# Layer 1 of an MLP in Strassen's seven products, on one Trainium2 core

## The chip, the core and the metric

The kernel runs on one core of a Trainium2 chip. The core has a matrix engine (PE, TensorE; its weight loads are shown apart as PEld), a vector engine (DVE), a scalar engine (ACT), a general engine (POOL, GpSimd) and a queue that issues the DMAs (SP). The metric is the device time of one execution in microseconds (us). Numbers of the profile come from one profiled execution.

## What is computed

Performer attention, a low-rank mixing of tokens, and a relu MLP with a residual; all in float32, with the weights given in float64.

```python
# q, k, v: (8 batches, 8 heads, 576 tokens, 64); omega: (128, 64)
phi(x) = exp(h - max(h)) / sqrt(m)        # h = scaled x @ omega^T - |x|^2 / 2
attn = phi(q) (phi(k)^T v) / (phi(q) sum(phi(k)) + 1e-6)
x = attn as (8, 576, 512)
u = x + (x^T U V)^T                       # U: (576, 32), V: (32, 576)
out = u + relu(u @ w1) @ w2               # w1: (512, 2048), w2: (2048, 512)
```

## The kernel before

The 8 x 576 rows make 36 tiles of 128 tokens. The program has three stages: the attention and the mixing, which write u to DRAM (tensors `u_dram`); a first part of the MLP during which the float64 weights are still decoded (five DVE instructions, two of POOL and two of ACT for each of 32 pieces of 512 columns, lines 111 to 163); and the rest of the MLP with all weights in place. The MLP is the larger part of the program.

A float32 product on PE is made of three passes over operands that are split into a rounded high part and a remainder (float32r): high x high, low x high, high x low. A split is a cast on ACT and a subtraction on POOL. `w1` is kept split for good in `w1h` and `w1l`, `w2` in `w2s`.

The MLP takes u in 12 chunks of three tiles (384 tokens; `CT = 3`, class `Chunk`). For a chunk, 32 x 32 blocks are fetched from `u_dram` by 16 DMAs into four buffers `uraw` (line 327), turned on DVE into `uT` (line 672), cast on ACT into `uh` (675) and subtracted on POOL into `ul` (676). An item is a chunk c and a block f of 128 of the 2048 hidden columns (16 blocks):

- `layer1`: 12 matmuls of 384 columns into one PSUM bank `p_p` (lines 682 to 684), then relu on ACT into `gh` (687) and the remainder on DVE into `gl` (688);
- `layer2`: for each of three tiles three matmuls of 512 columns, summed over all f in the chunk's own banks (700).

PE does `layer1` of the next item before `layer2` of this one, so `gh` and `gl` have a whole layer 2 in which to be made. Chunks 0 and 1 share the pass over f while the weights are decoded. At a chunk's end DVE adds the residual rows of u (716), which SP has loaded into buffers of their own half a chunk earlier (711), and SP stores them (717).

The order on each engine is fixed when the program is built: a list scheduler of the framework places each instruction by its own estimate of times; only the instructions marked with `keep_in_program_order` hold the order of the source among themselves. Each engine then takes its instructions strictly in that order.

Of the kernel before, what the change touches and what calls it, by code (L numbers as in the profile page):

```python
# [23 lines left out]
#: High words of the least and the greatest float64 with a normal float32's exponent.  # L24
# [4 lines left out]
def performer_mlp_kernel(ctx: ExitStack, tc, q, k, v, omega, U, V, w1, w2, out):  # L29
    """phi(q) (phi(k)^T v) / den, then x + V^T U^T x and a relu MLP with a residual.  # L30

    float32 products run natively or as float32r passes over operands split exactly into a
    rounded high part and the remainder. U, V, w1 and w2 come as the bits of float64 and are
    rounded to float32. The 2 x 576 rows of a pair of batches make nine tiles of 128, the fifth
    with the last 64 rows of one batch and the first 64 of the next.
    """
    nc = tc.nc
# [16 lines left out]
    # Both feature maps carry 1 / sqrt(M), which the quotient drops when the guard grows by M.  # L54
# [12 lines left out]
    CT = 3  # L67
    NCH = NP * NT // CT
    TOK = CT * P
    u_dram = [dram.tile([TOK, DM], F32, name=f"u_dram{i}") for i in range(NCH)]  # L70
# [26 lines left out]
    def decoding(jobs, late=0):  # L97
        """jobs: (load, n, finish...); load(raw) fills [P, n, 2] with the words of n float64 in each
        row, and each finish(w) runs in turn on the float32 [P, n]. Yields after every VectorE
        instruction; loads run ahead."""  # L100
# [18 lines left out]
        for i, job in enumerate(jobs):  # L119
# [4 lines left out]
            # The float32 of the high word's bits in m; the rest is the low word in units of 2^-52  # L124
            # of its power of two.
# [40 lines left out]
    def w1_job(i):  # L166
        f, c = divmod(i, NC)
        fs = slice(f * PIECE, (f + 1) * PIECE)
        return weights(w1[c * P : (c + 1) * P, fs], lambda: (w1h[:, c, fs], w1l[:, c, fs]))

    # What the first steps of the MLP need, then the pieces of w1 and w2 in turn.
# [16 lines left out]
    # U in columns [high, high, low, high], a slot for each tile of each batch: four of the first  # L188
    # batch, the shared tile's two with zeros in the other batch's rows, four of the second.
# [22 lines left out]
    # V in rows [high, high, high, low]; the shared tile has a slot for each batch.  # L212
# [27 lines left out]
    # Instructions of the decoder before the first that needs the late part of w2.  # L240
# [9 lines left out]
    def mixing(pair, x, last):  # L250
        """A tile of x may be written as late as the one before it is used. The last pair's has the
        more of VectorE and of the banks."""
# [21 lines left out]
        def add(t):  # L274
            ut = mp.tile([P, DM], F32, name="ut", tag="ut", bufs=2)
            nc.vector.tensor_tensor(out=ut, in0=sums.pop(t), in1=x[:, t, :], op=ALU.add)
            c, r = divmod(pair * NT + t, CT)
            stores.append((u_dram[c][r * P : (r + 1) * P, :], ut))
# [42 lines left out]
    def fetch(c, raws):  # L321
        """A chunk of u in 32 x 32 blocks that VectorE turns: row 32 a + i holds, for each block of 32
        tokens, 32 channels of block a of its token i."""
        for cc, raw in enumerate(raws):
# [13 lines left out]
    # The third unit comes before the first buffer is free; the second of x is, till then.  # L338
# [466 lines left out]
```

## Time and profile before

| | us |
|---|---|
| runs: median of 3 (lowest, highest) | 1155.97 (1155.81, 1158.91) |
| profiled execution, span of the trace | 1154.0 |
| PE busy in it | 1123.9 |
| DVE busy | 538.6 |
| ACT busy | 405.3 |
| POOL busy | 280.7 |

The profiled execution's own time is given as its span alone. In 40 slices of the span, PE is at 90% or more in nearly all; DVE is at 90% or more in slices of the attention and of the decoding (up to 450 us) and at 10 to 20% afterwards, ACT and POOL lower still. A row of a group reads: line, engine, operation, output<-inputs, shape, xcount | busy us, mean ns of one | idle time before, and what ended it.

### The profile page before, as it was taken

The page shows a single profiled execution, that of the slowest core. Times are in us where ns is not written, and L with a number is a line of the kernel's source. Part 1 is how long each engine was busy: PE and PEld are TensorE (multiplying, and loading weights), DVE is VectorE, ACT ScalarE, POOL GpSimd, SP SyncE. Part 2 cuts the span into 40 slices and gives each one's busy share as a digit, 9 for nine tenths or more (in the row PEclk, how much of TensorE's full clock was granted, in tenths as well). Part 3 has the DMA queues.
Part 4 walks back from the last instruction along what each step waited for, and adds up shares of the span by engine and source line. Part 5 has one row for each costly group of instructions (what it writes and reads, how often), then busy time and mean ns, then how long its engine had stood idle before and what let it go on. Part 6 is the DMA issues. An engine that isn't in the chain of part 4 may idle for free.

```text
span 1154.0 us, 17600 instructions
## 1 busy us (share of the span) xinstructions
PE 1123.9 (97%) x6481; PEld 1020.8 (88%) x6481; DVE 538.6 (47%) x1088; ACT 405.3 (35%) x1115; POOL 280.7 (24%) x261
## 2 busy tenths in 40 slices
PE   8989999999999889999999999999999999999998
PEld 7989889899978677999999999999999999999997
DVE  3889999998997998411212121221212121111211
ACT  4978889788842333211111111111111111111111
POOL 3446657645244555201001010100101010010000
PEclk7999999999999999999999999999999999999999
DMA  7787686774356332420303030030303001010100
GB/s 131 141 152 138 139 180 132 155 157 89 93 146 154 106 106 74 105 61 5 78 1 83 1 74 10 7 75 1 83 1 82 1 1 55 1 55 1 46 1 28
DMA packets 288661, 84.95 MB, mean 74 GB/s; under 512 B 270368, under 2 KB 270368, under 8 KB 288576
## 3 DMA queue, kind: packets, MB, share of 16 engines
q1 hardware_dynamic: 288512, 83.77, 31.8%
q8 instruction: 51, 0.84, 0.3%
q14 instruction: 34, 0.28, 0.1%
q0 software_dynamic: 64, 0.07, 0.0%
HBM read 64.91 MB, written 18.87 MB: 73 GB/s over the span
## 4 chain that ended last, share of the span: by engine, by line
PE 71%; DVE 10%; DMA 2%; issue 1%; SPq 1%; ACT 1%; POOL 0%; DVEq 0%; ACTq 0%
PE p_p L683 10%; PE p_n L700 10%; PE p_p L684 10%; PE p_p L682 10%; PE p_q L700 10%; PE p_m L700 5%; PE p_kv L700 5%; PE p_n L458 2%; DVE mag L131 2%; PE p_kv L412 2%; DVE de L134 2%; DVE mag L128 2%; PE p_p L500 1%; PE p_q L438 1%; PE p_p L502 1%
## 5 line engine op out<-in xcount | busy, mean ns | idle before, releaser
L688 DVE SCALAR_TENSOR_TENSOR gl<-p_p,gh 128x384 fp32r<-128x384 f32 x192 | 106.8, 556 | 522.2 <-ACT gh L687 521.9
L687 ACT ACTIVATE gh<-p_p 128x384 fp32r<-128x384 f32 x192 | 94.0, 490 | 570.1 <-PE p_p L684 569.1
L682 PE MATMUL p_p<-uh,w1h 128*128 128x384 f32 x768 | 258.5, 337 | 1.7 <-DVE gl L688 1.3
L683 PE MATMUL p_p<-uh,w1l 128*128 128x384 f32 x768 | 258.8, 337 | 0.0
L684 PE MATMUL p_p<-ul,w1h 128*128 128x384 f32 x768 | 258.1, 337 | 0.0
L515 ACT ACTIVATE e<-p_p,nm 128x128 f32<-128x128 f32 x576 | 166.4, 385 | 39.8 <-DVE nm L508 30.7
L676 POOL TENSOR_TENSOR ul<-uT,uh 128x384 fp32r<-128x384 f32 x48 | 48.4, 1039 | 537.2 <-ACT uh L675 537.2
L682 PEld LDWEIGHTS p_p<-uh,w1h 128*128 128x128 f32 x768 | 144.2, 188 | 11.2 <-DVE gl L688 2.0
L683 PEld LDWEIGHTS p_p<-uh,w1l 128*128 128x128 f32 x768 | 144.1, 188 | 9.1
L684 PEld LDWEIGHTS p_p<-ul,w1h 128*128 128x128 f32 x768 | 144.0, 188 | 0.3
L381 POOL TENSOR_TENSOR xl<-xT,xh 128x384 fp32r<-128x384 f32 x96 | 102.4, 1083 | 125.5 <-ACT xh L377 92.8
L508 DVE TENSOR_REDUCE nm<-p_p 128x4 f32<-128x512 f32 x144 | 98.1, 682 | 23.7 <-PE p_p L502 14.5
L500 PE MATMUL p_p<-omh,xh 128*128 128x256 f32 x288 | 94.2, 327 | 1.2 <-ACT e L515 0.9
L501 PE MATMUL p_p<-oml,xh 128*128 128x256 f32 x288 | 82.4, 286 | 0.0
L502 PE MATMUL p_p<-omh,xl 128*128 128x256 f32 x288 | 82.3, 286 | 0.0
L458 PE MATMUL p_n<-kv,eT 128*128 128x65 f32 x512 | 74.7, 273 | 7.1 <-DVE eT L443 3.3
L700 PE MATMUL p_n<-w2h,gl 128*128 128x512 f32 x192 | 76.6, 399 | 3.4 <-DVE gl L688 3.3
L458 PEld LDWEIGHTS p_n<-kv,eT 128*128 128x128 f32 x512 | 68.5, 193 | 12.0 <-DVE eT L443 6.4
L700 PE MATMUL p_n<-w2h,gh 128*128 128x512 f32 x192 | 75.8, 395 | 1.9 <-ACT gh L687 1.1
L700 PE MATMUL p_n<-w2l,gh 128*128 128x512 f32 x192 | 75.8, 395 | 0.3 <-POOL w2l L163 0.2
L700 PE MATMUL p_q<-w2l,gh 128*128 128x512 f32 x192 | 75.1, 392 | 0.0
L700 PE MATMUL p_q<-w2h,gl 128*128 128x512 f32 x192 | 75.0, 395 | 0.0
(106 smaller groups left out, 1863.4 us busy)
## 6 DMA issues: line engine op xcount, KB each, us to landing
raw<-in_moe_w_ch_dram SPq DMA_DIRECT2D x32, 512.0 KB, 3.8
u_dram<-ut SPq DMA_DIRECT2D x36, 256.0 KB, 2.3
u<-u_dram SPq DMA_DIRECT2D x36, 256.0 KB, 3.8
out_dram<-u SPq DMA_DIRECT2D x36, 256.0 KB, 2.5
kt<-in_k_dram SPq DMA_DIRECT2D x120, 72.0 KB, 2.6
qt<-in_q_dram SPq DMA_DIRECT2D x120, 72.0 KB, 2.7
uraw<-u_dram SPq DMA_DIRECT2D x176, 48.0 KB, 2.3
vt<-in_v_dram SPq DMA_DIRECT2D x60, 128.0 KB, 2.7
```

The costliest lines, as they stand in the source:

```text
L381: nc.gpsimd.tensor_tensor(out=self.xl[-1], in0=self.turned, in1=f32(self.xh[-1]), op=ALU.subtract)
L458: nc.tensor.matmul(pn[:, h, :], eT[:, h, :], kv[:, h, s // 5, :], start=True, stop=True)
L500: nc.tensor.matmul(o, part.xh[g][:, ts], oh, start=True, stop=False)
L502: nc.tensor.matmul(o, part.xl[g][:, ts], oh, start=False, stop=True)
L508: nc.vector.tensor_reduce(out=self.nm[:, :n], in_=self.pp[:, :n], axis=AX.X, op=ALU.max, negate=True)
L515: nc.scalar.activation(out=self.e[:, j, :], in_=self.pp[:, j, :], func=AF.Exp, bias=self.nm[:, j : j + 1])
L682: nc.tensor.matmul(ph, w1h[:, cc, fs], self.uh[cc], start=(cc == 0), stop=False)
L683: nc.tensor.matmul(ph, w1l[:, cc, fs], self.uh[cc], start=False, stop=False)
L684: nc.tensor.matmul(ph, w1h[:, cc, fs], self.ul[cc], start=False, stop=(cc == NC - 1))
L687: nc.scalar.activation(out=self.gh, in_=ph, func=AF.Relu)
L688: nc.vector.scalar_tensor_tensor(out=self.gl, in0=ph, scalar=0.0, in1=f32(self.gh), op0=ALU.max, op1=ALU.subtract)
L700: step = nc.tensor.matmul(po, g[:, ts], w, start=(f + i == 0), stop=(f == NF - 1 and i == 2))
```

## The change

- Chunks become 6, then seven times 4, then 2 tiles (`ends`); the first and the last are done as before, 512 or 256 tokens to a matmul of layer 1 (`whole1`).
- The seven chunks of 512 tokens do layer 1 for two blocks f and f + 8 at once, p = 0 to 7 (a "step" below), with the 2 x 2 block product (two halves of the 512 channels, two halves of the tokens, two blocks of w1) in seven products instead of eight. A product is six matmuls of 256 columns (two blocks of 128 channels, three passes). The products add up in PSUM where they can: X (products 0 and 3), Y (1 and 4), Z (2 and 6), W (5). DVE and ACT combine them (`after`): `p1` = X, `u2` = Y + p1, later `u3` = Y + p1, `c22` = Z + u3, `c21` = W + u3, `c12` = Z + u2, with relu (ACT) and remainder (DVE) on X, c22, c21 and c12 into `g`. Here c22 must have read Z before product 6 adds to it.
- The operands of the products are sums of blocks: four sums of w1 blocks (`ws`, DVE) and seven splits (`wx`, ACT and POOL) of 256 columns in every step; four sums of u blocks (`us`, DVE) and seven splits (`ux`) of 512 columns once in a chunk, in the last step of the chunk before, as the eight buffers `ux` come free product by product.
- `w1` stays in one float32 array `w1f`; the first and last chunk split two 256-column operands of it for each f (`Halves`).
- Layer 2 of a step runs between the products of the next step, three or four matmuls after each product (`between`, `take`).
- Residual rows of u use two buffers (`u`, tag `mag`); the third and fourth tile's rows are loaded after the first and second tile's have been stored (`late`).

```diff
-    CT = 3
-    NCH = NP * NT // CT
+    CT, TOK = 4, 4 * P
+    ends = [6, *range(10, NP * NT, CT), NP * NT]
...
-    w1h = const.tile([P, NC, DF], F32R, name="w1h")
-    w1l = const.tile([P, NC, DF], F32R, name="w1l")
+    w1f = const.tile([P, NC, DF], F32, name="w1f")
...
+    def split(hl, x):
+        nc.scalar.copy(out=hl[:, 0], in_=x)
+        nc.gpsimd.tensor_tensor(out=hl[:, 1], in0=x, in1=f32(hl[:, 0]), op=SUBTRACT)
...
+    class Weights:
+        def sum(self, i, a, b, op):
+            self.s[i] = up.tile([P, 2, P], F32, name="ws", bufs=4)
+            sums(self.s[i], a, b, op)
+        def add(self):
+            i, blk = len(self.ops), self.block
+            if i == 0:
+                x = blk(0, 0)
+            elif i == 1:
+                self.sum(1, blk(0, 1), blk(1, 1), ADD)
+                self.sum(2, self.s[1], blk(0, 0), SUBTRACT)
+                x = self.s[2]
+            elif i == 2:
+                x = self.s[1]
...
+            self.ops.append(two("wx", up, P, 8))
+            split(self.ops[-1], x)
...
+        def sum(self, i, a, b, op, out=None):
+            self.s[i] = up.tile([P, 2, HT], F32, name="us", bufs=2) if out is None else out
...
+        def products(self, w, between):
+            X, Y, Z, W = bank("p_p", 2), bank("p_p", 2), bank("p_m", 1), bank("p_kv", 1)
...
+            def after(i):
+                if i == 0:
+                    nc.scalar.copy(out=p1, in_=X)
+                elif i == 1:
+                    sums(u2, Y, p1, ADD)
+                elif i == 3:
+                    self.relu(g[0], t1, X)
+                elif i == 4:
+                    sums(u3, Y, p1, ADD)
+                    sums(c22, Z, u3, ADD)
+                elif i == 5:
+                    sums(c21, W, u3, ADD)
+                    self.relu(g[1], t1, c21)
+                    self.relu(g[1], t2, c22)
+                elif i == 6:
+                    sums(c12, Z, u2, ADD)
+                    self.relu(g[0], t2, c12)
+            for i, o in enumerate((X, Y, Z, X, Y, W, Z)):
+                x, wt = self.ops[i], w.ops[i]
+                for k in range(2):
+                    for j, (l, r) in enumerate(passes((wt[:, 0, k], wt[:, 1, k]), (x[:, 0, k], x[:, 1, k]))):
+                        tc.keep_in_program_order(nc.tensor.matmul(o, l, r, ...
+                after(i)
+                between(i)
...
+                if end:
+                    self.store(t, po)
+                    for late in order[m + 2 : m + 3]:
+                        self.residual(late)
+        def residual(self, t):
+            self.u[t] = dec.tile([P, DM], F32, name="u", tag="mag", bufs=2)
+            nc.sync.dma_start(out=self.u[t], in_=u_rows(first[self.c] + t))
...
+            def between(i):
+                take(steps, 4 - i % 2)
+                if new:
+                    new.add()
+                if p == NH - 1 and i < 6:
+                    if not short:
+                        nxt.add()
```

What stands on the engines, first on PE in the middle of the MLP. Before, an item:

```order
L682 MATMUL p_p<-uh,w1h 128x384
L683 MATMUL p_p<-uh,w1l 128x384
L684 MATMUL p_p<-ul,w1h 128x384
L700 MATMUL p_n<-w2h_5688,gh 128x512 [waits Activation_49]
L700 MATMUL p_n<-w2l_5689,gh 128x512
```

Now, the last product of one step and the first of the next, with layer 2 between them (`p_s` is a product's bank):

```order
L856 MATMUL p_s<-ux,wx 128x256 [waits DVE_49]
L856 MATMUL p_s<-ux,wx 128x256 [waits Pool_49] x2
L856 MATMUL p_s<-ux,wx 128x256 x3
L878 MATMUL p_q<-w2h_5637,g 128x512
L878 MATMUL p_q<-w2l_5638,g 128x512
L878 MATMUL p_q<-w2h_5637,g 128x512
L856 MATMUL p_s<-ux,wx 128x256 x2
```

The twelve long matmuls of a layer 1 have become groups of six shorter ones, and the first of product 6 waits for DVE (c22 and Z). On DVE, before, at a chunk's end (the next chunk's turns, one remainder `gl` for each f, and the adds of the residual together):

```order
L672 STREAM_TRANSPOSE uT<-uraw 128x384 [waits DMAHW6_49,DMAHW3_49,DMAHW7_49,DMAHW2_49,Pool_49]
L688 SCALAR_TENSOR_TENSOR gl<-p_p,gh 128x384 [waits Activation_49]
L716 TENSOR_TENSOR u<-p_n,u 128x512 [waits PE_49]
L716 TENSOR_TENSOR u<-p_q,u 128x512 [waits DMAHW5_49,DMAHW1_49,PE_49]
L716 TENSOR_TENSOR u<-p_q,u 128x512 [waits DMAHW0_49,PE_49]
L688 SCALAR_TENSOR_TENSOR gl<-p_p,gh 128x384 [waits Activation_49] x14
```

Now, DVE in the last step of a chunk (p = 7), from `u2` to `c22` (`near<-p_s,near` is u2, later u3; `far<-p_s,near` is c22):

```order
L679 TENSOR_TENSOR near<-p_s,near 128x256 [waits PE_49,Activation_49]
L679 TENSOR_TENSOR us<-uT,us 128x512 [waits Pool_49]
L679 TENSOR_TENSOR ws<-w1f 128x256 [waits Pool_49]
L679 TENSOR_TENSOR us<-uT 128x512 [waits Pool_49]
L817 SCALAR_TENSOR_TENSOR g<-p_s,g 128x256 [waits Activation_49]
L679 TENSOR_TENSOR ws<-ws,w1f 128x256 [waits DVE_49,Pool_49]
L679 TENSOR_TENSOR near<-p_s,near 128x256 [waits PE_49]
L679 TENSOR_TENSOR far<-p_s,near 128x256 [waits DVE_49]
```

Three sums that wait for POOL have come ahead of u3 and c22. And the step after it (p = 0 of the next chunk), from the row behind `u2` to `c22`; the adds `u<-p_n,u` and `u<-p_q,u` are the residual of the chunk before:

```order
L894 TENSOR_TENSOR u<-p_n,u 128x512 [waits DMAHW5_49,DMAHW0_49,PE_49]
L752 STREAM_TRANSPOSE uT<-uraw 128x512 [waits DMAHW6_49,DMAHW4_49,DMAHW7_49,DMAHW3_49,Pool_49]
L752 STREAM_TRANSPOSE uT<-uraw 128x512 [waits DMAHW3_49,DMAHW4_49,DMAHW2_49,DMAHW1_49]
L679 TENSOR_TENSOR ws<-w1f,ws 128x256 [waits Pool_49]
L679 TENSOR_TENSOR us<-uT 128x512 [waits DVE_49]
L679 TENSOR_TENSOR ws<-w1f 128x256 [waits DVE_49,Pool_49]
L894 TENSOR_TENSOR u<-p_n,u 128x512 [waits DMAHW5_49,DMAHW0_49,PE_49]
L817 SCALAR_TENSOR_TENSOR g<-p_s,g 128x256 [waits Activation_49]
L679 TENSOR_TENSOR ws<-ws,w1f 128x256 [waits DVE_49,Pool_49]
L679 TENSOR_TENSOR near<-p_s,near 128x256 [waits PE_49]
L894 TENSOR_TENSOR u<-p_q,u 128x512 [waits DMAHW6_49,DMAHW2_49,PE_49]
L679 TENSOR_TENSOR far<-p_s,near 128x256 [waits DVE_49]
```

The adds, which stood side by side, are now spread among the sums, and the third of them (`u<-p_q,u`, whose rows are loaded late) stands directly ahead of c22.

More of the change, by code (lines that the diff above doesn't have):

```diff
@@ L757, in performer_mlp_kernel @@
-    for _ in range(NC):
-        chunks[1].turn()
+        if n % 2 and one.turned < NC:
+            one.turn()
+            one.whole()
+            if one.turned == NC:
+                g = begin()
+    g = g or begin()
     while left[0] > 0:
@@ new lines, in performer_mlp_kernel, with each @@
+    pairs, nxt = Weights(0), Chunk(1)
+    def each(f):
+        advance(decoder, 10, True)
+        if 8 <= f < 12:
+            nxt.fetch()
+            nxt.turn()
+        if f == 12:
+            nxt.prepare()
+        if 13 <= f < 15:
+            nxt.add()
+        if f == NF - 1:
+            one.residual(4)
+            one.residual(5)
+            for i in range(7):
+                pairs.add()
+                if len(nxt.ops) < 7:
+                    nxt.add()
+    steps = whole_pass(one, g, each)
@@ L778, with each @@
+    g = nxt.whole1(ws.pop(0))
+    take(steps)
+    def each(f):
+        if f == NF - 1:
+            nxt.residual(0)
+            nxt.residual(1)
+    take(whole_pass(nxt, g, each))
 _INS = ['q', 'k', 'v', 'omega', 'moe_U', 'moe_V', 'moe_w_ch1', 'moe_w_ch2']
```

276 lines of the change are left out of this document (185 added, 91 removed).

## The prediction

> **What bounds the kernel now.** I read the page's head and its chain of waits first, then the busy time by stretch of the span, then single instructions in the timeline.
>
> ```profile
> span 1154.0 us, 17600 instructions
> PE 1123.9 (97%) x6481; PEld 1020.8 (88%) x6481; DVE 538.6 (47%) x1088; ACT 405.3 (35%) x1115; POOL 280.7 (24%) x261
> PE 71%; DVE 10%; DMA 2%; issue 1%; SPq 1%; ACT 1%; POOL 0%; DVEq 0%; ACTq 0%
> ```
>
> PE is the bound; only 30 us of the span are without it. Where it waits, and for whom, the stretches tell (columns: busy us and count on PE, PEld, DVE, ACT, POOL; granted clock; DMA share; GB/s):
>
> ```profile
> 320.00:400.00 80.00, 75.15 (x366) 63.03 (x365) 70.69 (x114) 29.61 (x59) 40.84 (x32) 1.00 0.54 141
> 400.00:460.00 60.00, 52.26 (x246) 42.97 (x245) 55.66 (x71) 19.64 (x36) 34.61 (x25) 1.00 0.30 91
> 480.00:1148.00 668.00, 668.00 (x3363) 606.02 (x3362) 126.72 (x224) 94.50 (x191) 31.98 (x33) 1.00 0.14 35
> ```
>
> In the last row PE never rests, at full granted clock, while DVE works 19% and POOL 5%: whatever shortens the stream of matmuls shortens the program, as long as the idle engines can feed it. From 320 to 460 DVE is at 88 to 93% and PE has holes: there the decoding is the bound. The stream itself, in the timeline (start, duration):
>
> ```profile
> 601.46 0.33 PE L682 MATMUL p_p<-uh,w1h 128*128 128x384 f32 x1
> 601.63 0.33 PE L683 MATMUL p_p<-uh,w1l 128*128 128x384 f32 x1
> ...
> 603.54 0.39 PE L700 MATMUL p_m<-w2h,gh 128*128 128x512 f32 x1
> 603.77 0.39 PE L700 MATMUL p_m<-w2l,gh 128*128 128x512 f32 x1
> ...
> 605.61 0.34 PE L682 MATMUL p_p<-uh,w1h 128*128 128x384 f32 x1
> ```
>
> Starts count, not durations, since matmuls overlap: twelve of 384 columns take 603.54 − 601.46 = 2.08 us (0.174 each), nine of 512 take 2.07 (0.230 each), an item 4.15. By the window it is 668.00 × 21 / 3363 = 4.17; I use that.
>
> **What PE saves.** A step of the new kernel does four tiles and two blocks, the work of 8/3 items, so 11.12 us before. It has 42 matmuls of 256 columns and 24 of 512. The attention shows the short ones in a row:
>
> ```profile
> 239.96 0.28 PE L500 MATMUL p_p<-omh,xh 128*128 128x256 f32 x1
> ...
> 240.08 0.28 PE L501 MATMUL p_p<-oml,xh 128*128 128x256 f32 x1
> ...
> 240.20 0.28 PE L502 MATMUL p_p<-omh,xl 128*128 128x256 f32 x1
> ...
> 240.44 0.19 PEld L502 LDWEIGHTS p_p<-omh,xl 128*128 128x128 f32 x1
> 240.55 0.28 PE L502 MATMUL p_p<-omh,xl 128*128 128x256 f32 x1
> 240.56 0.53 PEld L412 LDWEIGHTS p_kv<-vm,e 128*128 128x128 f32 x4
> ```
>
> Five steps from 239.96 to 240.55 are 0.118 each. The four loads at the end, 0.19 each, take 0.53 in all, so they begin (0.53 − 0.19) / 3 = 0.113 apart: a 256-column matmul just covers its weight load. A step is 42 × 0.118 + 24 × 0.230 = 10.48 us, say 10.50: 0.62 less. Seven chunks of eight steps: 56 × 0.62 = **−35 us**. The six-tile chunk takes 12 × 0.230 + 12 × 0.118 + 18 × 0.230 = 8.32 per block against 2 × 4.17, the two-tile chunk 2.80 against 2.78: nothing. One product in eight saved in layer 1 is thus mostly there, and the rest of the question is what waits.
>
> **Feeding an ordinary step.** Durations by form:
>
> ```profile
> L676 POOL TENSOR_TENSOR ul<-uT,uh 128x384 fp32r<-128x384 f32 x48 | 48.4, 1039 | 537.2 <-ACT uh L675 537.2
> L149 POOL TENSOR_TENSOR mag<-mag,de 128x512 f32<-128x512 f32 x32 | 43.2, 1351 | 40.1 <-DVE de L135 38.4 <-DVE rec L469 1.6
> L443 DVE COPY eT<-p_q 128x256 f32<-128x256 f32 x79 | 32.4, 410 | 4.3 <-PE p_q L438 4.0
> L483 DVE TENSOR_TENSOR x<-p_n,rec 128x256 f32<-128x256 f32 x64 | 26.5, 416 | 0.8
> L443 ACT COPY eT<-p_q 128x256 f32<-128x256 f32 x65 | 25.5, 393 | 9.8 <-PE p_q L438 9.8
> L672 DVE STREAM_TRANSPOSE uT<-uraw 128x384 f32<-128x384 f32 x44 | 25.3, 575 | 35.6 <-POOL ul L676 31.1 <-DMA uraw<-u_dram 3.9 <-issue 0.5
> ```
>
> POOL costs (1351 − 1039) / 128 = 2.4 ns a column, so 0.73 us for 256 columns: seven `wx` splits are 5.1 of 10.5 us. DVE has thirteen operations of 256 columns (four `ws`, u2, u3, c22, c21, c12, four remainders) at 0.41: 5.4. ACT has seven casts, p1 and four relus at 0.39: 4.7. All fit, and `wx` is made a step ahead, so the splits themselves cost nothing: idle POOL covers them. The tight place is c22 ahead of product 6. With three or four matmuls between products, these start at 0, 1.63, 3.03, 4.66, 6.06, 7.68 and 9.08. Product 4 ends at about 7.0; then u3, one `ws`, c22 on DVE: 7.0 + 3 × 0.41 = 8.25 against 9.08. I take no stall.
>
> DVE can be slower than that beside POOL:
>
> ```profile
> 315.63 0.68 DVE L261 TENSOR_TENSOR ml<-x,mh 128x512 fp32r<-128x512 f32 x1
> ...
> 327.55 3.87 POOL L676 TENSOR_TENSOR ul<-uT,uh 128x384 fp32r<-128x384 f32 x3 [16.94 <-ACT uh L675]
> 327.68 1.44 DVE L261 TENSOR_TENSOR ml<-x,mh 128x512 fp32r<-128x512 f32 x1
> ...
> 329.04 0.68 DVE L276 TENSOR_TENSOR ut<-ph,x 128x512 f32<-128x512 f32 x1
> ...
> 404.35 1.29 POOL L163 TENSOR_TENSOR w1l<-mag,w1h 128x512 fp32r<-128x512 f32 x1 [0.73 <-ACT w1h L162]
> 404.39 1.80 DVE L131 SCALAR_TENSOR_TENSOR mag<-raw,mag 128x512 uint32<-128x512 uint32 x1
> ```
>
> The same subtraction (261) takes 0.68 alone and 1.44 when a POOL operation has just begun; the decoding's L131 takes 1.80, ending 0.55 us after POOL's 404.35 + 1.29. L276, whose first input is in PSUM, keeps its 0.68 within POOL's 3.87. So a DVE operation with both inputs in SBUF waits out POOL's running one, and as POOL's three took 3.87 for 3 × 1.04, POOL waits for DVE too. The sums `ws`, `us` are of that kind; u3 and c22, which read PSUM, are not. In an ordinary step one such wait is at most 0.73, so c22 comes by 8.98 at the latest: still no stall, but barely.
>
> The Trainium skill, page "SBUF — State Buffer", section "Who interferes with whom", gives this as a rule: DVE and GpSimd share one pair of ports, taken exclusively for a whole instruction, and a DVE instruction with two SBUF inputs contends with a GpSimd one that reads SBUF. The trace agrees (0.68 against 1.44). By the rule the terms for the chunk's ends below stand; without it the first of them would be nothing, and the sum 9 us lower.
>
> **The chunk's last step (p = 7), six times.** POOL gets six `ux` splits of 512 columns more (1.35 each) beside seven of 0.73: 13.2 us of work in a step of 10.5, with waits for DVE about 14. DVE's row there is u2, `us`, `ws`, `us`, a remainder, `ws`, u3, c22, and `us` and `ws` wait for POOL to be done with what their buffers held. Without collisions: u2 is done at 3.0, the `us` goes when the third `ux` split is through (3.3), the `ws` behind a `wx` and a `ux` split at 6.0 to 6.6, then `us` 0.7, remainder 0.41, `ws` 0.41, u3, c22: 8.6, no stall. With two collisions of 0.7 to 1.35 it is 10.5 to 11.5, and product 6 goes 1.4 to 2.4 late. Bounds 0 and 2.5; I take 1.5, nearer to the upper since POOL is busy without a break there: 6 × 1.5 = **+9**.
>
> **The step after it (p = 0), five times.** The third residual add (`u<-p_q,u`) stands right ahead of c22, and its rows are loaded only when the first tile has been stored.
>
> ```profile
> u<-u_dram SPq DMA_DIRECT2D x36, 256.0 KB, 3.8
> out_dram<-u SPq DMA_DIRECT2D x36, 256.0 KB, 2.5
> ...
> L716 DVE TENSOR_TENSOR u<-p_n,u 128x512 f32<-128x512 f32 x12 | 8.3, 689 | 0.3 <-DMA u<-u_dram 0.2
> ...
> DMA to landing us min/median/max: 2.0/3.0/4.9
> ```
>
> Before, both transfers were off the path, loaded half a chunk ahead. Now: the old chunk's first tile is summed at about 2.8, added by 3.7 (0.69 and queueing); its store lands 2.0 to 2.5 later (5.7 to 6.2); SP then issues the load, which lands 2.5 to 3.8 later (8.2 to 10.0); add 0.69, c22 0.41: 9.3 to 11.1 against 9.08. DVE's own queue, with two transposes of 512 columns (0.575 × 512 / 384 = 0.77 each), three sums and a POOL wait or two, gives 8.7 to 12.2 by itself. Stall 0.2 to 3.1; middle, somewhat up for the DVE side, 2.3: 5 × 2.3 = **+11.5**. In the sixth such step that add stands behind c22: **+1**. On SP's queue only the fetches of the chunk after next stand behind these stores and loads, and they aren't needed for some 30 us: nothing lost there.
>
> **The first pass.** Chunk 0 runs during the decoding, where DVE is the bound. The decode's own pieces stay; POOL's splits of `w1` (one of 512 per block) become two of 256 and cost the same. DVE has the transposes of six tiles as before, but also the first `us` and `ws` of chunk 1 in the last block: 11 sums of 0.41 to 0.7, about 6 us, part of it in PE's shade. Bounds −2 (PE's work there orders itself better) and +6; I take **+2**, and another **+2** (0 to 3) for the turn from chunk 0 to 1, whose operands all wait for residual and transposes at once. The last turn (to the two-tile chunk) has only half as many splits: 0.
>
> Sum: −35 + 9 + 11.5 + 1 + 2 + 2 = −9.5, from the profiled span 1154.0 to 1144.5. The runs' median, 1155.97, lies 2.0 above that span, so the runs should show 1146.5; I say 1146.
>
> **Rivals.**
> 1. The ends of chunks cost little, since POOL's extra splits lag into the next step without anyone waiting and the third add comes in time (2.0 + 2.5 after the first). For it: every term there has a lower bound near 0. Against it: POOL's 13.2 us in 10.5, which must be made up. Time: −35 with 0 to 10 us of waits, 1121 to 1131.
> 2. The other side: product 6's wait for c22 in every ordinary step. Its slack is 0.1 to 0.8 us, and a late remainder or an added signal's delay of a few tenths uses it up. The 56 steps less twelve at the turns are 44; 0.22 us lost in each already cancels the −9.5, and 0.3 to 0.6 each (a single collision with POOL beyond what I allow) is +13 to +26: 1159 to 1172. Against it: DVE is only half full in these steps.
> 3. The 256-column matmuls don't hold 0.118 among changing weights: at 0.128 each, 56 × 42 × 0.010 = 24 us go and the time is 1170. For it: the load of 0.113 leaves 5 ns. Against it: the quoted rows run at that rate with the weights changed at each matmul.
>
> **Chances.** Forecast (gain less waits at the turns) 0.52: within it the eleven waits, 20.5 us or 1.9 each, lie between 0.6 and 2.4, which is 1132 to 1152. The rest: rival 1, 0.20; rival 2, 0.20; rival 3, 0.05; something else that slows it, 0.03. What a measurement of this kernel can tell from no change is about 0.3%, 3.5 us. Faster takes rival 1 and most of the forecast: 0.69. Between 1152.5 and 1159.5 lies the upper edge of the forecast and the lower of rival 2: 0.13. Slower: 0.18. The range goes from 1123, leaving out the best of rival 1, to 1164, inside rival 2; the forecast's own is 1132 to 1152.
>
> **What would show it.** Starts of L856 0.12 apart and ordinary steps 10.5 us long would show the −35; longer starts, rival 3. The waits list should have "PE p_s L856 <- DVE far" at product 6, six times some 84 us apart in p = 7 and p = 0 with 1 to 3 us each, with DVE's `us` and `ws` (L679) idle for POOL, and `u` (L894) idle for the DMA; if the same wait comes 40 times or more, rival 2; if it sums to under 5 us, rival 1. Wrong as a whole would be a PE with long holes in 320 to 480, or a chunk 0 that takes over 10 us longer.

## The result, and the profile after

The changed kernel is slower: 1170.53 us (median of 4 runs, 1169.01 to 1175.16) against 1156.31 (the kernel before, now 4 runs), ratio 1.0124 with a 95% interval of 1.0100 to 1.0148. The forecast was 1146, the range 1123 to 1164. The profiled execution of the changed kernel has a span of 1167.0, 13.0 more than before. Head and chain of its page:

```profile
span 1167.0 us, 20841 instructions
PE 1111.7 (95%) x7105; PEld 993.3 (85%) x7105; DVE 813.0 (70%) x1692; ACT 615.8 (53%) x1716; POOL 644.0 (55%) x710
PE 64%; DVE 16%; DMA 8%; issue 4%; SPq 3%; POOL 3%; ACT 2%; DVEq 0%; POOLq 0%; ACTq 0%
```

PE is busy 12 us less, in a span 13 us longer: it waits some 25 us more. DVE now stands for 16% of the chain. By stretch (busy us and count on PE, PEld, DVE, ACT, POOL; granted clock; DMA share; GB/s):

```profile
320.00:490.00 170.00, 153.87 (x724) 125.11 (x723) 139.68 (x206) 68.30 (x145) 100.77 (x89) 0.94 0.34 94
560.00:1000.00 440.00, 424.79 (x2600) 377.51 (x2600) 281.67 (x571) 196.95 (x507) 265.01 (x311) 0.99 0.15 36
```

Before, the first of them had a granted clock of 1.00, and from 480 on PE had no gap. Now PE loses 15 us of 440 among the steps, and the first pass ran with a clock of 0.94. What PE waits for from 480 to the end:

```profile
PE p_s L856 <- DVE far L679: 17.4, 7, 3.1
PE p_q L878 <- DVE u L894: 1.8, 1, 1.8
```

The first row is the seven steps p = 0, product 6 waiting for c22 (`far`); the second is layer 2 in p = 1 of chunk 1, which waits for an add of the residual. The start times of PE's matmuls in the trace give the length of each step: an ordinary one 10.64 us, a last one (p = 7) 10.87, a first one (p = 0) 14.1 to 15.5 from chunk 2 to 6. Added up along the program, against the same work before:

- the MLP's first matmul is 4.7 us later (332.26 against 327.52);
- the first pass, to the same state of the work, takes 157.4 us against 150.8: +6.6;
- the 56 steps, priced by their matmuls, take 56 x 10.62 = 595 against 56 x 11.12 = 623: −28; their waits and the stretches of low clock behind these are 22.8 + 6.4 = +29;
- the chunk of two tiles at the end: +0.9.

The sum is 13.4, where the spans differ by 13.0. The saving in matmuls is there, and is used up at the turns from chunk to chunk, mostly by DVE's row; what makes the kernel slower than before lies ahead of the steps. The MLP's first matmul, now and before:

```profile
332.26 0.50 PE L810 MATMUL p_p<-ux,wx 128*128 128x512 f32 x1 [2.77 <-ACT ux L675]
327.52 0.44 PE L682 MATMUL p_p<-uh,w1h 128*128 128x384 f32 x1 [0.39 <-ACT uh L675]
```

DVE's row at the turn from chunk 3 to 4 (timeline; product 6 could have begun near 769.4):

```profile
763.95 0.41 DVE L679 TENSOR_TENSOR near<-p_s,near 128x256 f32<-128x256 f32 x1
764.28 0.67 DVE L894 TENSOR_TENSOR u<-p_n,u 128x512 f32<-128x512 f32 x1
764.88 1.28 DVE L752 STREAM_TRANSPOSE uT<-uraw 128x512 f32<-128x512 f32 x2
766.10 0.90 DVE L679 TENSOR_TENSOR ws<-w1f,ws 128x256 f32<-128x256 f32 x1
766.92 1.22 DVE L679 TENSOR_TENSOR us<-uT 128x512 f32<-128x512 f32 x1
768.07 1.51 DVE L679 TENSOR_TENSOR ws<-w1f 128x256 f32<-128x256 f32 x1
769.51 0.68 DVE L894 TENSOR_TENSOR u<-p_n,u 128x512 f32<-128x512 f32 x1
770.11 0.41 DVE L817 SCALAR_TENSOR_TENSOR g<-p_s,g 128x256 fp32r<-128x256 f32 x1
770.44 0.69 DVE L679 TENSOR_TENSOR ws<-ws,w1f 128x256 f32<-128x256 f32 x1
771.06 0.41 DVE L679 TENSOR_TENSOR near<-p_s,near 128x256 f32<-128x256 f32 x1
771.39 0.67 DVE L894 TENSOR_TENSOR u<-p_q,u 128x512 f32<-128x512 f32 x1
771.99 0.41 DVE L679 TENSOR_TENSOR far<-p_s,near 128x256 f32<-128x256 f32 x1
```

No row has an idle time in brackets: DVE is busy without a break from u2 to c22, and the third add (771.39) waits for no load. The sums stretch (`ws` 0.41 to 0.90 and 1.51, `us` 0.69 to 1.22) while those that read PSUM do not. POOL at the same place:

```profile
766.68 0.92 POOL L676 TENSOR_TENSOR wx<-w1f,wx 128x256 fp32r<-128x256 f32 x1
767.56 1.74 POOL L676 TENSOR_TENSOR ux<-uT,ux 128x512 fp32r<-128x512 f32 x1
769.26 0.90 POOL L676 TENSOR_TENSOR wx<-ws,wx 128x256 fp32r<-128x256 f32 x1
```

The `ws` of 768.07 ends at 769.58, after POOL's `ux` split has ended at 769.30.

### The profile page after: what moved, and what is told of

Its sections match the earlier page's. It is cut to its first block, busy times and chain, and to the rows that moved or that the text cites. A ratio compares the mean times of both kernels' runs of the same rounds, so it can differ in the third digit from the quotient of the medians.

```text
span 1167.0 us, 20841 instructions
## 1 busy us (share of the span) xinstructions
PE 1111.7 (95%) x7105; PEld 993.3 (85%) x7105; DVE 813.0 (70%) x1692; ACT 615.8 (53%) x1716; POOL 644.0 (55%) x710
## 4 chain that ended last, share of the span: by engine, by line
PE 64%; DVE 16%; DMA 8%; issue 4%; SPq 3%; POOL 3%; ACT 2%; DVEq 0%; POOLq 0%; ACTq 0%
PE p_s L856 19%; PE p_n L878 13%; PE p_q L878 11%; PE p_p L810 4%; PE p_n L463 3%; PE p_kv L417 3%; DVE ws L679 3%; PE p_p L505 2%; DMA raw<-in_moe_w_ch_dram 2%; DMA u<-u_dram 2%; SPq L358 2%; DVE g L817 2%; PE p_p L507 2%; PE p_p L506 2%; PE p_q L443 2%
## 5 line engine op out<-in xcount | busy, mean ns | idle before, releaser
L856 PEld LDWEIGHTS p_s<-ux,wx 128*128 128x128 f32 x2352 | 336.6, 191 | 56.3 <-DVE far L679 22.7
L856 PE MATMUL p_s<-ux,wx 128*128 128x256 f32 x2352 | 348.1, 284 | 17.4 <-DVE far L679 17.4
L676 POOL TENSOR_TENSOR wx<-w1f,wx 128x256 fp32r<-128x256 f32 x232 | 184.3, 798 | 140.0 <-ACT wx L675 125.0
L676 POOL TENSOR_TENSOR wx<-ws,wx 128x256 fp32r<-128x256 f32 x224 | 173.7, 776 | 154.7 <-ACT wx L675 154.7
L878 PE MATMUL p_n<-w2h,g 128*128 128x512 f32 x576 | 198.1, 401 | 0.4
L878 PE MATMUL p_q<-w2h,g 128*128 128x512 f32 x512 | 191.9, 398 | 1.8 <-DVE u L894 1.8
L878 PEld LDWEIGHTS p_n<-w2h,g 128*128 128x128 f32 x576 | 109.7, 191 | 17.9 <-DVE g L817 2.4
L810 PE MATMUL p_p<-ux,wx 128*128 128x256 f32 (+1 forms) x576 | 105.8, 336 | 15.0 <-DVE g L817 11.0
L878 PE MATMUL p_n<-w2l,g 128*128 128x512 f32 x288 | 115.0, 399 | 0.0
L878 PEld LDWEIGHTS p_q<-w2h,g 128*128 128x128 f32 x512 | 93.6, 191 | 12.2 <-DVE u L894 2.0
L878 PE MATMUL p_q<-w2l,g 128*128 128x512 f32 x256 | 101.7, 397 | 0.0
```

Source lines behind the costliest of these rows:

```text
L676: nc.gpsimd.tensor_tensor(out=hl[:, 1], in0=x, in1=f32(hl[:, 0]), op=SUBTRACT)
L810: nc.tensor.matmul(ph, l, r, start=(cc + i == 0), stop=(cc == NC - 1 and i == 2))
L856: tc.keep_in_program_order(nc.tensor.matmul(o, l, r, start=(i in (0, 1, 2, 5) and k + j == 0), stop=(k == 1 and j == 2), skip_group_check= ...
L878: tc.keep_in_program_order(nc.tensor.matmul(po, l, r, start=(begin and n + i == 0), stop=(end and n == len(fs) - 1 and i == 2)))
```

## The experiments

Each is the changed kernel but for its diff, unless another is named. Where only one time is given, it is a single run; the kernel before, beside them on the same chips, had medians of 1156.3 to 1156.8. "Step" lengths and "the first pass" (first matmul of the MLP to first product) are from the traces.

**u4: the residual's rows in four buffers.**

```diff
-                    for late in order[m + 2 : m + 3]:
+                    for late in order[m + 2 : m + 3] if self.n > CT else []:
...
-            self.u[t] = dec.tile([P, DM], F32, name="u", tag="mag", bufs=2)
+            pool, tag = (rp, "u") if self.n == CT and t in (2, 3) else (dec, "mag")
+            self.u[t] = pool.tile([P, DM], F32, name="u", tag=tag, bufs=2)
...
                 now.residual(0)
                 now.residual(1)
+                now.residual(2)
+                now.residual(3)
```

(`rp` is a new pool of two buffers)

> The residual rows of a chunk of four tiles have four buffers and are loaded together, so the third add waits for no load; DVE's order around it is nearly as in the changed kernel. Theory A (DVE's row of work from u2 to c22 is itself too long): product 6 of the steps p = 0 still waits 2.5 to 3.5 us for c22, and the time is within 5 us of the changed kernel's 1170. Rival B (the late load holds the third add and with it c22): these waits, 17 us in seven steps, are gone or under 0.7 each, and the time is about 1153.

1181.18 us. DVE's order did not stay as it was: the scheduler put a transpose between u3 and c22, and the waits grew to 3.7 us. But the third add waits for no load here, and in the changed kernel's own trace it waits 0.05 us at most in the steps p = 0 of chunks 2 to 6. So the late load is not the cause at these turns; A holds.

```profile
773.26 0.41 DVE L680 TENSOR_TENSOR near<-p_s,near 128x256 f32<-128x256 f32 x1
773.60 0.69 DVE L753 STREAM_TRANSPOSE uT<-uraw 128x512 f32<-128x512 f32 x1
774.22 0.64 DVE L896 TENSOR_TENSOR u<-p_q,u 128x512 f32<-128x512 f32 x1
774.79 0.40 DVE L680 TENSOR_TENSOR far<-p_s,near 128x256 f32<-128x256 f32 x1
```

**order_steps: DVE in the order of the source from chunk 1 on.**

```diff
+    held = [False]
+    def hold(step):
+        if held[0]:
+            tc.keep_in_program_order(step)
...
-        nc.vector.tensor_tensor(out=out, in0=a, in1=b, op=op)
+        hold(nc.vector.tensor_tensor(out=out, in0=a, in1=b, op=op))
...
     steps = whole_pass(one, g, each)
+    held[0] = True
```

(and so for the remainders, the adds of the residual and the transposes)

> From chunk 1 on DVE's instructions hold the order of the source: the transposes go back to p = 3 to 6, the third add stands behind c22, the sums of w1 behind the combination. Late loads stay. Theory A: the waits of product 6 in p = 0 (17.4 us) go, and with them the 6.4 us at half clock that follow: 1146 to 1150. Rival B: the third add, now behind c22, is as late as before and holds its bank, so that layer 2 of p = 1 waits for it, 1 to 3 us five times: 1152 to 1162. Ordinary steps stay at 10.64 us; if the fixed order delays c22 in them, some 0.2 us more for each.

1168.79 us, ratio 1.0115 (1.0099 to 1.0130). Neither: the transposes are gone from p = 0, yet 2.0 us of wait stay there (the step takes 13.45), and p = 7 now takes 11.36, a loss of 3.5 per chunk, about as with the scheduler's order (0.2 and 3.5). What stands before c22 is less now, but starts later: at the turn from chunk 3 to 4, u2 starts 6.1 us into the step, against 4.1 in the changed kernel.

**dve_order: the same in the first pass.** DVE's instructions hold the order of the source from the start (`keep_in_program_order` at the same four places, without the condition).

> As the run before, and DVE's remainders, sums and transposes of the first pass too hold the order of the source, which puts the remainders of a block behind its ten operations of decoding and not behind more. Theory A (order): the four waits of about 3 us of layer 1 for the remainder, and the four stretches of half clock that follow them (7.3 us), go: some 8 us less than the run before, 1138 to 1143. Rival C (the pass is bound by the sum of DVE's work, whatever its order): within 3 us of the run before.

1172.93 us, ratio 1.0131 (1.0094 to 1.0168). Rival C holds: the first pass takes 157.7 us. The waits of about 3 to 4 us became nine of 1.0 to 2.4 and one of 3.6; the time at half clock from the start of the MLP fell from 20.5 to 13.7 us, and the waits in sum rose by about what that gave back.

**calm: w1's operands made once.** `new.ops = pairs.ops` in every step. The expectation speaks of once per chunk, but `pairs` is carried on from chunk to chunk, so that all 56 steps use the operands made in the first pass (`ws<-w1f` stands twice in the trace, not 112 times); the kernel leaves out all others.

> All steps of a chunk use the operands of w1 that the chunk's first step made: the four sums and seven splits of w1 per step are left out from the second step on, so POOL, ACT and DVE do about half of their work in an ordinary step. Theory D (the matmuls are a little slower beside busy engines): a 512-column matmul of layer 2 goes back from 0.2335 to 0.230 us, a 256-column one from 0.1199 to 0.118, a step from 10.64 to 10.48. Rival E (the price lies in the matmuls themselves): 10.64 stays. The waits of product 6 in p = 0 shrink to under 1.5 us each by either, as DVE's row loses three sums and POOL most of its splits.

1161.61 us. Rival E: the step stays at 10.64, with 0.2337 and 0.1194 per matmul (means, without the waits), as in the changed kernel (0.2336 and 0.1194). The price is not made by busy neighbours: POOL is busy for 49 of 440 us here (560 to 1000), against 265. Waits in p = 0 of 1.6 to 2.8 us stayed, longer than either theory had it. They have another cause: at the turn from chunk 3 to 4 the scheduler put transposes ahead of c22 whose rows SP fetches only then, and DVE stands idle for them for 1.70 and 1.85 us.

**w1_sub: the attention's order put back.**

```diff
+        if i < 7:
+            job += (lambda w: nc.gpsimd.tensor_tensor(out=w, in0=w, in1=w1f[:, c, fs], op=ALU.subtract),)
```

> The changed kernel, with one POOL subtraction of 512 columns (in place, its result unused) put back behind each of the first seven decoded pieces of w1, as the kernel before had there for its split; that gives the engines the order of the attention that they had before. Theory F (the attention became longer because its instructions were put in another order): the 48 exponentials from number 288 to 336 take 25.4 us as before, not 27.8, and the MLP begins 2 to 4 us earlier than in the changed kernel (332.3). Rival G (the attention varies by itself between executions): 27.8 stays, or the start stays within 332 to 338.

1174.24 us. The 48 exponentials took 25.5 us (172.6 to 198.1), so F holds for that place: by leaving out POOL's split of w1, the change let the scheduler rearrange the attention, at a cost of 2.3 us (27.8 in the changed kernel and in every other run of it). But the MLP began at 331.8, only 0.5 earlier: the part ahead of these exponentials took 0.9 longer, and between the runs of this study, which begin the MLP between 330.0 and 339.7, that part varies by more than this term. From the end of the last exponential to the MLP's first matmul it is 9.1 us here as in the changed kernel (9.1 to 10.1 in all its variants), against 6.7 before. The first pass (159.6) and the 56 steps (628.4 against 624.7) were longer in this run, so the time says nothing of F.

**ux_blank: POOL writes zeros at a chunk's end, reads nothing** (from order_steps).

```diff
-            split(self.slot(), x)
+            hl = self.slot()
+            nc.scalar.copy(out=hl[:, 0], in_=x)
+            nc.gpsimd.memset(f32(hl[:, 1]), 0.0)
```

> order_steps, but POOL writes zeros into the low halves of the seven splits of u sums instead of subtracting (the low x high pass is left out by that), so POOL reads nothing there. Theory H (DVE and POOL exclude each other, and the subtractions of u at a chunk's end are more than the shared path can take beside the sums): the losses of 0.7 us in p = 7 and 2.8 in p = 0 go to under 0.3 each; ws and us in these steps take 0.41 and 0.69 again unless they meet a wx split. 1168 becomes about 1148. Rival I (POOL's backlog alone, or DVE's own sum of work, delays the row): at least 2 us per chunk stay.

1145.74 us: all steps p = 7 and p = 0 from chunk 2 to 6 take 10.6 us. Of the 23 us, 21 lie in the 56 steps and 2 in the first pass, where the splits for chunk 1 are written as zeros too. The subtractions at a chunk's end are the cause. One writing is 0.53 us, though, so POOL is also less busy, and that is taken apart next.

**ux_blank3: the zeros written three times.**

> As the run with blank low halves of the u splits, but POOL writes the zeros three times (3 x 0.53 = 1.6 us per split, against 1.45 for the subtraction): POOL is as busy as with the subtractions, and still reads nothing for them. Theory H (exclusion between DVE's and POOL's reads): no loss at the turns, as with one writing, about 1146; ws and us as short as there. Rival I (POOL's backlog of work is what delays the row): 0.7 us in p = 7 and 2 or more in p = 0 come back, about 1166.

1141.57 us, and no wait of PE at the turns from chunk 1 to 2 on:

```profile
560.00:1000.00 440.00, 440.00 (x2735) 395.45 (x2734) 288.94 (x602) 198.99 (x535) 273.84 (x405) 1.00 0.15 36
```

The run to compare is order_steps, from which this one differs in the writings alone: the 56 steps take 601.9 us against 623.3 (of the rest of the 27 us, 4.3 is an earlier start of the MLP, which varies between runs). POOL is busier than there (273.84 against 262.57 us of 440), DVE about as busy (288.94 against 293.28), and PE never rests. The writings don't wait for ACT's cast as the subtractions must; but in order_steps, between 520 and 1085 us, POOL stands idle for no such cast and DVE for no buffer that POOL still reads, so this isn't what they gain. It is neither POOL's work nor DVE's alone that holds PE up, but that both read SBUF at once: theory H. The same `ws` in p = 0, with what POOL did beside it, first in order_steps, then here:

```profile
763.58 1.51 DVE L685 TENSOR_TENSOR ws<-w1f,ws 128x256 f32<-128x256 f32 x1
763.34 1.48 POOL L682 TENSOR_TENSOR ux<-uT,ux 128x512 fp32r<-128x512 f32 x1
...
663.03 0.42 DVE L685 TENSOR_TENSOR ws<-w1f,ws 128x256 f32<-128x256 f32 x1
662.41 2.39 POOL L805 MEMSET ux<- 128x512 f32 x5
```

The groups of instructions of order_steps and of this run, whole program:

```profile
L685 DVE TENSOR_TENSOR ws<-w1f 128x256 f32<-128x256 f32 x112 | 55.2, 493 | 0.0
L685 DVE TENSOR_TENSOR ws<-w1f,ws 128x256 f32<-128x256 f32 x56 | 30.5, 545 | 0.0
L685 DVE TENSOR_TENSOR us<-uT 128x512 f32<-128x512 f32 x14 | 14.8, 1060 | 6.1 <-POOL ux L682 6.1
```

```profile
L805 POOL MEMSET ux<- 128x512 f32 x147 | 72.4, 525 | 12.0 <-PE p_s L865 7.8 <-PE p_p L819 3.4
...
L685 DVE TENSOR_TENSOR ws<-w1f 128x256 f32<-128x256 f32 x112 | 51.8, 462 | 0.0
L685 DVE TENSOR_TENSOR ws<-w1f,ws 128x256 f32<-128x256 f32 x56 | 23.4, 418 | 0.0
L685 DVE TENSOR_TENSOR us<-uT 128x512 f32<-128x512 f32 x14 | 12.6, 897 | 4.7 <-ACT ux L803 4.7
```

A `us` falls from 1.06 to 0.90 in the mean, the `ws<-w1f,ws` from 0.55 to 0.42. What is left above 0.69 and 0.41 are the `wx` splits, which stayed: from 490 us on, a `us` that met only writings took 0.68 and a `ws` 0.42, and every one that took longer had met a subtraction.

**ux_dve: the seven subtractions on DVE** (from order_steps): `hold(nc.vector.tensor_tensor(out=hl[:, 1], in0=x, in1=f32(hl[:, 0]), op=SUBTRACT))` in place of the memset above.

> order_steps, with the seven subtractions of u sums per chunk on DVE (0.69 each by its rows of 512 columns) instead of POOL (1.35). Theory H: time on the shared path falls from 9.4 to 4.8 us per chunk, the losses at the turns from 3.5 to 1 us or less: 1152 to 1156. Rival I (DVE's own sum decides: 5.3 + 2.8 + 4.1 = 12.2 us in p = 7, 1.6 over the step): the losses stay at 2 to 4 us, 1162 to 1172.

1168.36 us, ratio 1.0105 (1.0078 to 1.0131). Rival I here: p = 0 fell to 11.4 to 11.7, but p = 7 rose to 13.2, in three chunks 14.0 to 14.4, a loss of 3.4 to 4.6. DVE's 12.2 us don't fit a step either.

**spread9: a ninth buffer, two splits a step earlier** (from order_steps).

```diff
-            self.ops.append(up.tile([P, 2, 2, HT], F32R, name="ux", bufs=8))
+            self.ops.append(up.tile([P, 2, 2, HT], F32R, name="ux", bufs=9))
...
+                if p == NH - 2 and i in (2, 4) and not short:
+                    nxt.add()
                 if p == NH - 1 and i < 6:
                     if not short:
-                        nxt.add()
+                        if i < 5:
+                            nxt.add()
```

> order_steps with nine buffers for the splits of u instead of eight, and two of a chunk's seven splits, with the sums before them, moved from the last step into the one before it. Theory H or I alike: the work of the turn is spread over one more step; the loss per chunk falls from 3.5 us to 1 to 2: 1154 to 1160. If the wait is not for this work but for the third add or for c22's own chain, 1168 stays.

1168.99 us, ratio 1.0099 (1.0074 to 1.0123). The loss per chunk fell, but to 2.5 us (p = 7 11.27, p = 0 12.45), not to 1 to 2; and the first pass took 162.4 us, in another order of instructions: the 56 steps gave back 7.1 us against order_steps, and the first pass took 5.2 of them.

**mix and mix_all: four of the seven subtractions on DVE as well** (from spread9; in mix_all `held = [True]`).

```diff
+            self.flush()
+            if self.c > 1 and i in (0, 1, 3, 5):
+                nc.scalar.copy(out=hl[:, 0], in_=x)
+                self.pend = (hl, x)
+            else:
+                split(hl, x)
```

(`flush` issues the waiting subtraction on DVE)

> Nine buffers and two splits moved ahead as in spread9, and from chunk 2 on four of the seven subtractions of u sums (the first two, the fourth and the sixth) on DVE, each placed behind the next split's sum; nothing left out. POOL then has 3 x 1.35 + 5.1 = 9.2 us in p = 7, DVE 5.3 + 1.4 + 1.4 = 8.1. Theory H: the loss per chunk falls from 2.5 us (spread9) to under 1: the 56 steps end within 608 us, and the time is 1152 to 1160, depending on the first pass (157 to 162 us). Rival I (DVE's own work decides): 2 us per chunk stay.

> As mix, with DVE's order of the source held in the first pass too, which keeps the sums for chunk 1 from coming ahead of the decoding: first pass 156 to 158 us instead of spread9's 162, and 3 to 6 us less than mix: 1148 to 1156. If the first pass is bound by the sum of DVE's and POOL's work, as the run dve_order spoke for, its length is the same as in mix within 2 us.

mix 1162.88 us, ratio 1.0051 (1.0034 to 1.0068); mix_all 1158.64, 1.0016 (1.0000 to 1.0032), not told from no change. The steps: p = 7 10.88, p = 0 12.1, a loss of 1.7 per chunk, where under 1 was expected, so nearer to Rival I's 2. First pass: 162.2 and 158.1 us. With DVE held, the sums for chunk 1 no longer come among the decoding.

**l2_f and g_two: the price of layer 2's matmuls.** l2_f swaps the loops over tiles and blocks in `second`; g_two makes `g` two tiles.

> The changed kernel with layer 2 of a step going through the tiles once for each of its two blocks, so that three matmuls in a row and not six add to one bank. Theory J (the 512-column matmul costs 0.2335 instead of 0.230 us because of six in a row to one bank): it falls to 0.230 to 0.232. Rival K (it lies in the operands themselves): 0.2335 stays. The time moves by at most 5 us either way, and by the turns, where DVE's order may change.

> The changed kernel with the rounded part and the remainder of the hidden values in tiles of their own, as the kernel before has gh and gl, and not in one tile g. Theory P (the price of 0.2336 us for a 512-column matmul of layer 2 comes from where its stationary operand lies): it goes to about 0.230. Rival Q: 0.2336 stays; the cause is then elsewhere and stays open.

l2_f: 1198.64 us; the tiles of a chunk finish later, layer 2 waits 16.9 us for adds of the residual, and p = 1 of chunks 2 to 6 takes 13.1 to 17.0 us. g_two: 1166.53. The means per 512-column matmul are 0.2339 and 0.2335. Both J and P fall; why it is not 0.2307, the kernel before's mean from 560 to 1080 us, stays open.

**halves_blank: the first pass without POOL's reads for w1.** In `Halves`, the subtraction becomes three memsets.

> The changed kernel, with the low half of w1 in the first and last chunk (two operands for each block f) written as zeros by POOL three times instead of subtracted, so that POOL is as busy there and reads nothing. Theory N (the splits of w1 at use, which exclude DVE's decoding, lengthen the first pass): from its first matmul to the first product it takes 153 us or less instead of 157.4. Rival O (POOL's adds of the decoding and DVE's own work bound it): 156 to 158 stay.

1177.46 us, first pass 165.1. Inconclusive: the memsets, which wait for no cast, were placed otherwise, and a stall of 6.1 us appeared at 339.7, in the mixing; without it some 159. Nothing in it speaks for N.

**best: what stands ahead of c22 moved behind it** (from mix_all).

```diff
                 elif i == 3:
-                    self.relu(g[0], t1, X)
+                    self.high(g[0], t1, X)
                 elif i == 4:
                     sums(u3, Y, p1, ADD)
                     sums(c22, Z, u3, ADD)
+                    self.low(g[0], t1, X)
...
             def between(i):
+                flush_stores()
                 take(steps, 4 - i % 2)
```

(`high` and `low` are the two halves of `relu`; the adds of finished tiles are kept until the next `flush_stores`)

> As mix_all, and in DVE's row the adds of finished tiles and the remainder of X go behind u3 and c22. Theory L (what is left of the loss in p = 0, 1.5 us, is what stands ahead of c22 there): p = 0 falls from 12.1 to 10.7 or 11, the 56 steps by about 8 us, 1158.6 to about 1150. Rival M (the rest is the late start of the row, from POOL's and DVE's work in p = 7): 12 us stay, 1157 to 1160.

1153.25 us (median of 12 runs), ratio 0.9970 with an interval of 0.9957 to 0.9984: faster than both kernels. Theory L: p = 0 fell from 12.1 to 11.2, though p = 7 rose to 11.05; the 56 steps take 6 us less than in mix_all. PE's waits from 480 on:

```profile
PE p_s L883 <- DVE far L685: 3.2, 8, 1.4
PE p_s L883 <- DVE u L921: 0.6, 1, 0.6
PE p_s L883 <- DVE near L685: 0.5, 2, 0.3
PE p_n L905 <- ACT g L840: 0.2, 1, 0.2
```

## Why the prediction was wrong

By its steps:

- **Matmuls, −35: measured −28.** The steps that fail are the two prices. A 256-column matmul starts 0.1194 after the last, not 0.118; the prediction had it from five rows of the attention. The line through the two other prices would have been the better source only with a long mean: 0.1747 at 384 columns (the kernel before from 560 to 1080 us) and 0.230 at 512 meet 256 at 0.1194, while the 0.174 that the prediction took from twelve starts leads to 0.118 as well. A 512-column one costs 0.2336 instead of 0.230. Together they are 7 us over the 56 steps. Rival 3 named the first, at 0.128; it was a seventh of that.
- **Ordinary steps, no stall: right.** 10.64 us throughout, and rival 2, to which 0.20 was given for the side on which the result fell, did not happen: c22 comes in time in all of them.
- **p = 7, +9: measured +1.4** (0.23 each). The collisions came, but the slack held; what they delayed was the next step.
- **p = 0, +11.5: measured +20 in these five** (waits of 3.1 us for c22, 0.35 each for layer 2 ahead of it, 2.5 of low clock in sum). The mechanism was half right. The third add does stand in the way, but for its own 0.67 us; its rows had landed in time (no idle time before it). DVE's own queue had been put at 8.7 to 12.2 us and c22 was taken at 11.4; it came at 12.6. That p = 7 and p = 0 draw on one resource, so that 14 us of POOL's reading in the one are paid in the other, is the step of thought that was missing. At the turn from chunk 3 to 4, only four of the seven `ux` splits ran in p = 7 and three, 4.7 us, in p = 0. ux_blank3 shows the resource. Nor were `ws` and `us` the only ones that meet POOL there: three of the four remainders have both inputs in SBUF too, and took 0.50 (c22, c12) and 0.71 (c21) in the mean from 490 to 1114 us, where the prediction had 0.41 and X's remainder, which reads PSUM, took 0.42. That the two terms for p = 7 and p = 0 came to 21.4 together, where 20.5 was forecast, is luck: one was 7.6 too high, the other 8.5 too low.
- **The turns from chunk 0 to 1 and from 6 to 7, +3: measured +7** (waits of 2.1 and 1.9 us with 1.6 of low clock at the first; 1.2 at the other).
- **The first pass, +2: measured +6.6.** The steps alone come out about even with before; this term and the next make the kernel slower. PE waits as long in sum as before (21 us from 325 on, against 20), but in pieces of 3 to 4 us in place of 0.3 to 1.4 (11.0 us in six waits for DVE's remainder `g`, the longest 3.9), and behind the long ones it runs at half rate: the granted clock is 0.50 for 20.5 us from 333.9 to 456.8, where before it was 1.00 throughout, which costs some 7 to 8 us by the starts of the matmuls. The prediction had no term for the clock at all. Why the waits come bundled was not taken apart: DVE in the order of the source (dve_order) split them, and the pass was no shorter.
- **The attention, 0: measured +4.7** at the MLP's start. 2.3 of it stand in the 48 exponentials and come from the new order (w1_sub takes them away). 2.4 stand between the last exponential and the MLP's first matmul (9.1 us against 6.7), in every run: the first chunk now has six tiles, whose transposes fill DVE from 328.6 to 332.4, and PE awaits ACT's cast of them for 2.8 us, against 0.4. These are two terms that the prediction left out without a reason; what varies between runs is the part ahead of both.

In spans, 1144.5 was forecast and 1167.0 came: 7 in the matmuls, 5.7 at the turns (29.2 against 23.5), 4.6 in the first pass, 4.7 ahead of it and 0.9 behind (22.9 where the spans say 22.5). No one term is the error; these five all erred to the same side, and the terms that were not examined (the attention, the clock) had been put at nothing.

## What to carry to other kernels

Work put on two idle engines is not free when both read SBUF: DVE at 64% and POOL at 60% (560 to 1000 us) got in each other's way here, and the price fell on the one instruction that PE waited for. Count such work over the two or three stages that share it, not stage by stage, and put what PE waits for first in its engine's row. And price a wait of PE by its length and place: many short ones cost what they are, a long one can cost a slow stretch behind it too; a change that bundles the same waiting into fewer, longer pieces can be slower for that alone.

## What the runs showed of the hardware

After a long wait PE's granted clock falls to half, for 3.41 us or a whole multiple of that. In the changed kernel such stretches begin at 333.89, 381.67, 412.39, 453.35, 501.14, 593.30 and 682.05, whole multiples of 3.413 us apart: the clock is granted in windows on a grid that the waits don't shift. Two windows of this grid, at a wait of 3.1 us that ended at 592.0, and two at an equal wait that ended at 772.4 (first column behind the length: PE busy; the granted clock is the third from the end):

```profile
589.89:593.30 3.41, 1.34 (x9) 1.25 (x10) 3.41 (x9) 0.69 (x2) 1.34 (x2) 1.00 0.72 201
593.30:596.71 3.41, 3.41 (x13) 2.93 (x12) 2.10 (x6) 1.55 (x5) 1.47 (x2) 0.50 0.78 168
767.39:770.80 3.41, 2.14 (x13) 1.53 (x11) 3.41 (x5) 0.72 (x3) 3.41 (x4) 1.00 0.75 156
770.80:774.21 3.41, 1.76 (x11) 1.63 (x12) 3.41 (x9) 1.10 (x3) 1.12 (x3) 1.00 0.81 213
```

The first wait left one window with 2.07 us idle, and in the next one 256-column matmuls started 0.21 apart. The second was cut by an edge into 1.27 and 1.65 us, and cost nothing more. The traces of the changed kernel and its fifteen variants, in the MLP (from 345 us to the last 20 us of each), bear this out: of the windows at full clock, all 70 in which PE stood idle for 1.89 us or more were followed by one at half clock, and none of the 3569 with less than 1.80; of the 17 between, seven were. Of the windows at half clock, all 17 with 0.63 us or more of idle were followed by another, none of the 78 with less. (In the attention, whose matmuls are shorter, some full windows with less idle, from 1.15 us, were followed by one too.)

So a wait's length decides only by chance. Among the turns of chunks 1 to 6, none of six waits of 2.0 us (order_steps) was followed by a slow stretch, three of six of 2.5 us (ux_dve), two of five of 3.1 to 3.3 us (the changed kernel), all five of 3.7 us (u4). A wait of 2.1 us at 500.3, which lay in one window, was followed by one as well.

The Trainium skill, page "TensorE: Matmul & The Clock Gate", Part 1, has the rule: the clock halves after an idle window of about 3.4 us and recovers after a busy one, and the window runs freely, so that it depends on where a wait falls in it. The trace agrees on the half rate, on the window of 3.41 us and on its running freely; but a window need not be idle throughout, 1.9 us of it were enough here.

The exclusion of DVE and POOL, which the prediction read from two rows, is confirmed as the cause of the turns' loss from chunk 1 to 2 on: with POOL only writing, it was gone although POOL was no less busy (273.84 us of 440 against 262.57). This is also what the Trainium skill's page "SBUF — State Buffer" states in "Who interferes with whom": a DVE instruction with two SBUF inputs contends with a GpSimd instruction that reads SBUF, not with one that only writes it.
